# An order planner for TensorE's matmuls, the PSUM banks of the first pass's experts, and the durations the planner assumes

## The chip, the cores and the metric

The kernel runs on one core of a Trainium2 chip. The metric is the time of one execution in microseconds (us) on the device. One execution was also taken with the hardware profiler, and all rows come from that one.

## The reference

Four sequences of 576 tokens with 8 heads of 64 go through retention, a softmax-gated layer with layer norm, and four experts whose outputs are summed with given weights. In short:

```python
scores = (q @ k.T) / sqrt(64)
x = (scores * decay_mask) @ v                    # 2304 tokens x 512
h = x @ w_in                                     # 512 -> 1024
solu = h * softmax(h)
ln = (solu - mean(solu)) / sqrt(var(solu) + 1e-6) * g_ln
x = ln @ w_out                                   # 1024 -> 512
for e in range(4):
    out += p[:, e:e + 1] * (relu(x @ w1[e]) @ w2[e])
```

All is float32. The kernel writes every large matmul as three, on the high and low parts of both operands (`mm3`, line 360).

## The kernel before

The 2304 tokens are 18 groups of 128, in three passes of six groups. A pass has four parts: attention and the first matmul `h_mm` of each group, with its softmax and norm chain on VectorE, ScalarE and GpSimd (`chain1` to `chain3b`) and transposes (`tr`); the second matmul `x2_mm`, whose results are split into sums and differences (`x2_new`); and the four experts. An expert has a first layer `l1` of four steps, each of seven products (a block scheme with seven in place of eight block products), and a second layer `l2_mm` or, in the later passes, two more such steps. Attention for the first eleven groups belongs to pass 0; the other seven groups (11 to 17, the list `OWN`) go beside the last expert's output tiles of pass 0 and beside the first matmuls of pass 1. The code counts passes from 0; the change's title says "pass one" for pass 0.

PSUM has eight banks of 512 f32 columns. In the kernel before, `bt` (b0, b1, b2) and `sbank` hold one each for the whole kernel, and the last four are a pool that is opened again and again: two double tiles `psA0` for pass 0, four single tiles `psX1`, `psX2` for the experts of the later passes (lines 1066 to 1075 and 1249), two double tiles `psA1` between them. `next_a` and `next_b` give these tiles in turn. In pass 0's experts a step takes x from `next_a` and y and z from `next_b` (line 909); products 1, 6, 4 and 7 go to x, 5 and 3 to y, and 2 to z. ScalarE and VectorE read them out: a copy or an add, then a ReLU on ScalarE (`relu_hi`), then its low part on VectorE (`relu_lo`). The second layer's output tiles take `next_b`, and VectorE adds them to `acc` (`l2_out`).

The first part of pass 0, up to about 98 us, is issued in the order of the string `ORDER`, written by hand. From `second(0)` on, instructions are recorded by `Recorder` and emitted at each `flush()`: a region is what lies between two flushes, and all of a region's instructions are emitted before those of the next. `flush` plans a region as a list schedule. Each operation has a cost from `FIXED` and `RATE`, a result reaches another engine after `LATENCY`, DMAs go one after the other at 300 GB/s with 2 us on top, and a PSUM bank takes one engine at a time. An operation's due time is the earlier of two: for a matmul its place on TensorE's clock in recorded order, and for any operation the due times of those that need it, less its cost. An engine takes the ready operation that is due first. TensorE alone may only take the next matmul in recorded order. All these instructions are issued from `op.call()`, so their line in the profile is 144, that of the recorded call; they are told apart by the names of their tiles. In the profile the tiles of `psA0` and `psA1` are psA and those of `psX1` and `psX2` are psX; h is the activation, wA and wC hold weights, wB the second matmul's or an expert's second weights, xa and xb the experts' inputs, tmp and dec attention data or scratch, acc the sums.

Of the kernel before, what the change touches and what calls it, by code (L numbers as in the profile page):

```python
# [59 lines left out]
l4 t5 r3 l5 s1 s3  # L60
"""

LATENCY = 0.12
ISSUE = 0.06
FIXED = {"PE": 0.0135, "ACT": 0.13, "DVE": 0.16, "POOL": 0.36, "SP": 2.0}
RATE = {"PE": 1 / 2400, "ACT": 0.93e-3, "DVE": 1.03e-3, "POOL": 1.82e-3, "SP": 4 * P / 300e3}
# [26 lines left out]
class Recorder:  # L93
# [32 lines left out]
    def record(self, name, engine, kind, args, kw):  # L126
        aps = dict(kw)
        aps.update(zip(("out", "in0", "in1") if kind == "matmul" else ("out", "in_"), args))
        outs = [aps[k] for k in ("out", "accum_out") if isinstance(aps.get(k), bass.AP)]
        keys = ("in_", "in0", "in1", "scalar", "scalar1", "scalar2", "bias", "scale")  # L130
        ins = [aps[k] for k in keys if isinstance(aps.get(k), bass.AP)]
        size = lambda ap: int(np.prod([d[1] for d in tuple(ap.ap)[1:]]))
        n = size(aps["out"])
        if engine == "SP" and aps["out"].space == bass.MemoryType.DRAM:
            n = size(aps["in_"])
        elif kind == "tensor_reduce":
            n = size(aps["in_"])
        rate = RATE[engine]
        if engine == "PE" and aps["in0"].dtype == F32:
            rate *= 2 if kw.get("is_transpose") else 4  # L140
        call = getattr(getattr(self.nc, name), kind)
        wide = [a for a in ins if a.space != bass.MemoryType.PSUM and size(a) > 1]
        port = engine == "POOL" or (engine == "DVE" and len(wide) > 1)
        op = Op(engine, lambda: call(*args, **kw), FIXED[engine] + rate * n, port)  # L144
        op.banks = {a.name for a in ins + outs if a.space == bass.MemoryType.PSUM}
        for a in ins:
            self.note(op, a, False)
        for a in outs:
            self.note(op, a, True)
        op.before.discard(op)  # L150
        op.index = self.count
        self.count += 1
        self.ops.append(op)

    def flush(self, done=True):
        ops, self.ops = self.ops, None if done else []
        clock = max(self.now, self.free["PE"])
        begin = clock
        inside = set(ops)
        for op in ops:  # L160
            op.after, op.due, op.at = [], None, clock
            if op.engine == "PE":
                op.due = clock
                clock += op.cost
        left, ready_at = {}, {}
        for op in ops:
            left[op], ready_at[op] = 0, 0.0
            for b in op.before:
                if b in inside:
                    b.after.append(op)  # L170
                    left[op] += 1
                else:
                    ready_at[op] = max(ready_at[op], b.end + (0 if b.engine == op.engine != "SP" else LATENCY))
        for op in reversed(ops):
            due = min((s.due for s in op.after), default=None)
            if due is None and op.engine != "PE":
                due = op.at + SLACK
            if due is not None:
                due -= op.cost + LATENCY
                op.due = due if op.due is None else min(op.due, due)  # L180
        free, busy = self.free, self.busy
        queue = {e: [] for e in FIXED}
        waiting, order = [], []
        pe = [op for op in ops if op.engine == "PE"]
        at, idle, now = 0, 0.0, self.now
        for op in ops:
            if not left[op]:
                heapq.heappush(waiting, (ready_at[op], op.index, op))
        while len(order) < len(ops):
            late = now + 1e-9  # L190
            while waiting and waiting[0][0] <= late:
                op = heapq.heappop(waiting)[2]
                queue[op.engine].append((op.due, op.index, op))
            moved = False
            for e in FIXED:
                if free[e] > late or not queue[e] or (e == "SP" and self.dma > late + DEPTH):
                    continue
                can = [r for r in queue[e] if not (r[2].port and self.port > late)]
                can = [r for r in can if all(busy.get(b, 0) <= late for b in r[2].banks)]
                if e == "PE":  # L200
                    can = [r for r in can if r[2] is pe[at]]
                if not can:
                    continue
                best = min(can)
                queue[e].remove(best)
                op = best[2]
                moved = True
                if e == "PE":
                    at += 1
                    idle += now - max(free[e], begin)  # L210
                if e == "SP":
                    free[e] = now + ISSUE
                    self.dma = max(self.dma, now) + op.cost - FIXED[e]
                    op.end = self.dma + FIXED[e]
                else:
                    op.end = free[e] = now + op.cost
                if op.port:
                    self.port = op.end
                for b in op.banks:
                    busy[b] = op.end if e == "PE" else op.end + LATENCY  # L220
                op.start = now
                order.append(op)
                for s in op.after:
                    left[s] -= 1
                    ready_at[s] = max(ready_at[s], op.end + (0 if s.engine == e != "SP" else LATENCY))
                    if not left[s]:
                        heapq.heappush(waiting, (ready_at[s], s.index, s))
            if not moved:
                times = [*free.values(), self.port, self.dma - DEPTH, *busy.values(), *(w[0] for w in waiting[:1])]
                now = min(t for t in times if t > late)  # L230
        self.now = min(free.values())
        if TRACE:
            print("scheduled %d from %.1f to %.1f (PE free %.1f) PE idle %.1f" % (len(ops), begin, self.now, free["PE"], idle))
            TRACE.append([(op.start, op.cost, op.engine, op.index, op.due) for op in order])
        for op in order:
            op.call()
# [11 lines left out]

SLACK = 12.0
DEPTH = 2.0  # L250
TRACE = []


@with_exitstack
def retention_solu_moe(
# [32 lines left out]

    bt = [psB.tile([P, 512], F32, tag=f"b{i}", name=f"b{i}") for i in range(3)]
    sbank = psB.tile([P, 512], F32, tag="s", name="sbank")  # L290
    turn = [0]
    open_pool("psA0", 2)

    def next_a():
# [3 lines left out]
    def next_b():  # L298
        turn[0] += 1
        return bt[turn[0] % 3]  # L300

    def quad(t):
        return t.rearrange("p (n t) -> p n t", n=4)
# [601 lines left out]
    def l1(s, i):  # L905

        m = s % NM
        if i == 1:
            x = next_a()[:, 0:BLK]
            y, z = (next_b()[:, 0:BLK] for _ in range(2))  # L910
            steps[s] = (x, y, z)
        x, y, z = steps[s]
        if i == 1:
            prod(s, 1, x)
            copy(t1r, x)
            if m > 0:
                relu_hi(1, m + 3, c22)
                relu_lo(1, m + 3, c22)
        elif i == 5:
            prod(s, 5, y)  # L920
            copy(t5r, y)
        elif i == 2:
            prod(s, 2, z)
            add(z, z, t1r)
        elif i == 6:
            prod(s, 6, x, True)
            copy(t2r, x)
            relu_hi(0, m, z)
            relu_lo(0, m, z)
        elif i == 3:  # L930
            prod(s, 3, y, True)
            add(y, y, t2r)
        elif i == 7:
            prod(s, 7, x, True)
            add(c22, x, t5r)
            relu_hi(1, m, y)
            relu_lo(1, m, y)
            if m == NM - 1:
                relu_hi(1, m + 4, c22)
                relu_lo(1, m + 4, c22)  # L940
        elif i == 4:
            prod(s, 4, x, True)
            relu_hi(0, m + 4, x)
            relu_lo(0, m + 4, x)
            steps.pop(s)
# [23 lines left out]
    def experts(p):  # L969
        for e in range(E):  # L970
# [9 lines left out]
                        l1(s - 1, 4)  # L980
                        w1_next(s + 2)
            last = s0 + NM - 1
            first = next_b()
            l2_mm(first, 1, 0, FORDER[:2], True, False)
            l1(last, 4)
            w1_next(last + 3)
# [10 lines left out]
            for b in (1, 0):  # L997
                for t in range(TB):
# [1 line left out]
                        ps, first = first, None  # L1000
                        l2_mm(ps, b, t, FORDER[2:], False, True)
                    else:
                        ps = next_b()
                        l2_mm(ps, b, t, FORDER, True, True)
                    l2_out(p, e, b * TB + t, ps)
                    if e + 1 == E:
# [59 lines left out]
    def experts_s(p):  # L1066
# [179 lines left out]
                        x_load(p + 1, g)  # L1246
        nc.flush()
        if p + 1 < NPASS:
            open_pool(f"psA{p}", 2)
            nc.start()  # L1250

    OWN = list(range(EARLY, NG))
# [32 lines left out]
    def second(p, g0):  # L1285

        if p == 0:
            raw = tmp[:, 2048:3072]
            w1_load(0)
            w1_load(1, raw)  # L1290
            xb_region()
            nc.start()
            w1_ops(0)
            w1_ops(1, raw)
# [20 lines left out]
    with tc.manual_schedule():  # L1315
# [43 lines left out]
            atoms[atom[0]](int(atom[1:]))  # L1359
        second(0, None)  # L1360
        experts(0)
        for p in range(1, NPASS):
            g0 = p * GP
            own = p == 1
# [119 lines left out]
```

## Time and profile before

| | us |
|---|---|
| median of 3 runs (1037.69 to 1041.31) | 1039.89 |
| profiled execution | 1042.08 |
| its span, first to last instruction | 1040.3 |
| TensorE busy | 1008.3 |
| VectorE busy | 617.3 |
| ScalarE busy | 526.9 |
| GpSimd busy | 445.6 |
| HBM traffic | 169.00 MB read, 62.95 MB written |

PE is TensorE's matmul, PEld its weight load (it overlaps matmuls), DVE is VectorE, ACT is ScalarE, POOL is GpSimd and SP is SyncE, which issues all DMAs. A row of a timeline has start, length, engine, source line, operation, out<-in, shapes and count, and in brackets the idle time before it and what ended it. Matmuls overlap each other in the rows, since each is shown with its whole latency: matmuls begin faster than one row's mean length suggests.

### The profile page before, as it was taken

The numbers are of one execution on the slowest core, as the hardware profiler recorded it, in microseconds if no ns is written. First come the engines' busy times: TensorE is split into PE (matmuls) and PEld (weight loads), VectorE is DVE, ScalarE is ACT, GpSimd is POOL, SyncE is SP. The second block draws the span as 40 slices with busy tenths as digits, with TensorE's granted clock in tenths as the row PEclk, the third lists the DMA queues.
The fourth block names the chain that finished last, engine by engine and source line by source line (L and its number), as shares of the span: only waits on it lengthen the run. The fifth ranks groups of instructions, "written<-read, shape, count | busy, mean of one in ns | idle before, by whom it ended". The sixth has DMA issues, their size and how long they took to land.

```text
span 1040.3 us, 17080 instructions
## 1 busy us (share of the span) xinstructions
PE 1008.3 (97%) x6188; PEld 947.0 (91%) x6188; DVE 617.3 (59%) x1038; ACT 526.9 (51%) x1032; POOL 445.6 (43%) x433
## 2 busy tenths in 40 slices
PE   4899999999999999999999999999999999999998
PEld 3788998898988987889999999999899999999998
DVE  6999686585774513643735656475444636556564
ACT  4568664262533402563745556473573746555462
POOL 2333354333635011321465655654230465655553
PEclk9999999999999999999999999999999999999999
DMA  9857689999785858551757666577640847566524
GB/s 343 343 186 257 216 293 313 309 292 336 227 270 185 280 226 304 203 200 59 232 152 226 184 195 211 157 270 248 243 152 18 250 134 244 163 216 193 184 72 134
DMA packets 122788, 226.79 MB, mean 218 GB/s; under 512 B 9936, under 2 KB 57040, under 8 KB 116560
## 3 DMA queue, kind: packets, MB, share of 16 engines
q1 hardware_dynamic: 122704, 225.70, 65.2%
q8 instruction: 49, 0.80, 0.3%
q14 instruction: 35, 0.29, 0.1%
HBM read 169.00 MB, written 62.95 MB: 223 GB/s over the span
## 4 chain that ended last, share of the span: by engine, by line
PE 51%; issue 1%; DVE 0%; ACT 0%; POOL 0%; POOLq 0%; ACTq 0%
PE psX L144 26%; PE b L144 16%; PE sbank L144 6%; PE psA L144 3%; DVE acc L144 0%; POOL acc L144 0%; DVE stats L144 0%; ACT psA L144 0%; ACT acc L144 0%; DVE tmp L144 0%; ACT xb L144 0%; ACT xa L144 0%; ACT tmp L144 0%; POOLq L144 0%; ACTq L144 0%
## 5 line engine op out<-in xcount | busy, mean ns | idle before, releaser
L144 POOL TENSOR_TENSOR h<-tmp,h 128x384 fp32r<-128x384 f32 x128 | 128.7, 1015 | 95.9 <-ACT h L144 82.1
L144 PE MATMUL b<-xa,wA 128*128 128x384 f32 x672 | 132.8, 335 | 2.3 <-DVE h L144 1.2
L144 PE MATMUL b<-wB,h 128*128 128x512 f32 x576 | 133.0, 390 | 1.3 <-POOL wB L144 1.3
L144 PEld LDWEIGHTS b<-wB,h 128*128 128x128 f32 x576 | 107.8, 188 | 24.2 <-POOL wB L144 2.2
L144 POOL TENSOR_TENSOR wA<-wA 128x512 fp32r<-128x512 f32 x74 | 97.2, 1321 | 68.0 <-ACT wA L144 65.0
L144 PEld LDWEIGHTS b<-xa,wA 128*128 128x128 f32 x672 | 117.7, 188 | 3.5 <-DVE h L144 2.1
L144 PE MATMUL psX<-xb,wA 128*128 128x384 f32 x576 | 112.6, 336 | 0.1
L144 PEld LDWEIGHTS psX<-xb,wA 128*128 128x128 f32 x576 | 100.4, 188 | 2.7 <-DVE b L144 2.3
L144 POOL TENSOR_TENSOR tmp<-tmp 128x256 f32<-128x256 f32 (+1 forms) x68 | 61.9, 925 | 72.0 <-DMA tmp<-in_w 50.0
L144 ACT ACTIVATE h<-tmp 128x384 fp32r<-128x384 f32 x144 | 72.9, 521 | 33.7 <-DVE tmp L144 33.7
L144 PE MATMUL b<-h,wB 128*128 128x384 f32 x480 | 85.1, 336 | 0.0
L144 PEld LDWEIGHTS b<-h,wB 128*128 128x128 f32 x480 | 83.0, 188 | 0.1
L144 PE MATMUL psX<-h,wA 128*128 128x384 f32 x408 | 74.9, 334 | 0.0
L144 DVE TENSOR_TENSOR sbank<-sbank,tmp 128x384 f32<-128x384 f32 x48 | 27.2, 566 | 77.4 <-PE sbank L144 54.3
L144 ACT ACTIVATE wA<-wA 128x512 fp32r<-128x512 f32 x74 | 46.3, 632 | 51.5 <-DMA wA<-sw 41.7
L144 ACT ACTIVATE tmp<-b 128x384 f32<-128x384 f32 x104 | 51.1, 491 | 41.8 <-DVE b L144 17.1
L144 PEld LDWEIGHTS psX<-h,wA 128*128 128x128 f32 x408 | 71.1, 188 | 0.0
L144 PE MATMUL psA<-wA,xa 128*128 128x512 f32 x288 | 70.2, 399 | 0.8 <-DVE tmp L144 0.7
L144 DVE TENSOR_TENSOR b<-b,tmp 128x384 f32<-128x384 f32 x80 | 45.0, 563 | 41.1 <-PE b L144 38.0
L144 PEld LDWEIGHTS psA<-wA,xa 128*128 128x128 f32 x288 | 53.6, 190 | 13.3 <-DVE tmp L144 1.0
L144 POOL TENSOR_TENSOR wC<-wC 128x512 fp32r<-128x512 f32 x38 | 50.6, 1337 | 31.8 <-ACT wC L144 31.8
L144 DVE SCALAR_TENSOR_TENSOR tmp<-b,tmp 128x384 f32<-128x384 f32 x96 | 51.2, 554 | 16.9 <-ACT tmp L144 8.5
(239 smaller groups left out, 1984.4 us busy)
## 6 DMA issues: line engine op xcount, KB each, us to landing
wA<-sw SPq DMA_DIRECT2D x298, 256.0 KB, 3.0
sw<-wA SPq DMA_DIRECT2D x32, 896.0 KB, 7.7
tmp<-in_w SPq DMA_DIRECT2D x24, 512.0 KB, 5.7
grps<-in_qkv SPq DMA_DIRECT2D x10, 1024.0 KB, 6.5
wC<-sw SPq DMA_DIRECT2D x38, 256.0 KB, 2.8
sw<-wCf SPq DMA_DIRECT2D x32, 256.0 KB, 3.3
wA<-sin SPq DMA_DIRECT2D x8, 1024.0 KB, 6.7
wB<-sout SPq DMA_DIRECT2D x8, 1024.0 KB, 8.0
```

The costliest lines, as they stand in the source:

```text
L144: op = Op(engine, lambda: call(*args, **kw), FIXED[engine] + rate * n, port)
```

## The change

The planner lets TensorE take, among the ready matmuls, the one that is due first, as long as it was recorded at most `AHEAD` = 150 operations (of any engine) behind the first matmul not yet issued. The assumed durations change: `LATENCY` from 0.12 to 0.15 us, f32 matmuls that are not transposes from four to two times a column's cost, and VectorE operations with two wide operands in SBUF to 1.2 times theirs. In pass 0's experts the two double tiles are given back before the region of `second(0)`, four single tiles `psX0` are opened, and x, y, z and the output tiles take all seven banks (three b, four psX0) in turn with `next_x`. Behind pass 0's experts there is a new flush, after which two double tiles `psA1` are opened for pass 1; those of pass 2 are now named `psA2`.

```diff
--- before.py
+++ after.py
@@ -60,7 +60,7 @@
 l4 t5 r3 l5 s1 s3
 """
 
-LATENCY = 0.12
+LATENCY = 0.15
 ISSUE = 0.06
 FIXED = {"PE": 0.0135, "ACT": 0.13, "DVE": 0.16, "POOL": 0.36, "SP": 2.0}
 RATE = {"PE": 1 / 2400, "ACT": 0.93e-3, "DVE": 1.03e-3, "POOL": 1.82e-3, "SP": 4 * P / 300e3}
@@ -137,10 +137,11 @@
             n = size(aps["in_"])
         rate = RATE[engine]
         if engine == "PE" and aps["in0"].dtype == F32:
-            rate *= 2 if kw.get("is_transpose") else 4
+            rate *= 2
         call = getattr(getattr(self.nc, name), kind)
         wide = [a for a in ins if a.space != bass.MemoryType.PSUM and size(a) > 1]
         port = engine == "POOL" or (engine == "DVE" and len(wide) > 1)
+        rate *= 1.2 if engine == "DVE" and port else 1.0
         op = Op(engine, lambda: call(*args, **kw), FIXED[engine] + rate * n, port)
         op.banks = {a.name for a in ins + outs if a.space == bass.MemoryType.PSUM}
         for a in ins:
@@ -158,7 +159,7 @@
         begin = clock
         inside = set(ops)
         for op in ops:
-            op.after, op.due, op.at = [], None, clock
+            op.after, op.due, op.at, op.start = [], None, clock, None
             if op.engine == "PE":
                 op.due = clock
                 clock += op.cost
@@ -198,7 +199,9 @@
                 can = [r for r in queue[e] if not (r[2].port and self.port > late)]
                 can = [r for r in can if all(busy.get(b, 0) <= late for b in r[2].banks)]
                 if e == "PE":
-                    can = [r for r in can if r[2] is pe[at]]
+                    while at < len(pe) and pe[at].start is not None:
+                        at += 1
+                    can = [r for r in can if r[2].index <= pe[at].index + AHEAD]
                 if not can:
                     continue
                 best = min(can)
@@ -206,7 +209,6 @@
                 op = best[2]
                 moved = True
                 if e == "PE":
-                    at += 1
                     idle += now - max(free[e], begin)
                 if e == "SP":
                     free[e] = now + ISSUE
@@ -248,6 +250,7 @@
 
 SLACK = 12.0
 DEPTH = 2.0
+AHEAD = 150
 TRACE = []
 
 
@@ -288,7 +291,7 @@
 
     bt = [psB.tile([P, 512], F32, tag=f"b{i}", name=f"b{i}") for i in range(3)]
     sbank = psB.tile([P, 512], F32, tag="s", name="sbank")
-    turn = [0]
+    turn = [0, 0]
     open_pool("psA0", 2)
 
     def next_a():
@@ -298,6 +301,10 @@
     def next_b():
         turn[0] += 1
         return bt[turn[0] % 3]
+
+    def next_x():
+        turn[1] += 1
+        return (bt + pool["a"])[turn[1] % 7]
 
     def quad(t):
         return t.rearrange("p (n t) -> p n t", n=4)
@@ -906,8 +913,7 @@
 
         m = s % NM
         if i == 1:
-            x = next_a()[:, 0:BLK]
-            y, z = (next_b()[:, 0:BLK] for _ in range(2))
+            x, y, z = (next_x()[:, 0:BLK] for _ in range(3))
             steps[s] = (x, y, z)
         x, y, z = steps[s]
         if i == 1:
@@ -980,7 +986,7 @@
                         l1(s - 1, 4)
                         w1_next(s + 2)
             last = s0 + NM - 1
-            first = next_b()
+            first = next_x()
             l2_mm(first, 1, 0, FORDER[:2], True, False)
             l1(last, 4)
             w1_next(last + 3)
@@ -1000,7 +1006,7 @@
                         ps, first = first, None
                         l2_mm(ps, b, t, FORDER[2:], False, True)
                     else:
-                        ps = next_b()
+                        ps = next_x()
                         l2_mm(ps, b, t, FORDER, True, True)
                     l2_out(p, e, b * TB + t, ps)
                     if e + 1 == E:
@@ -1246,7 +1252,7 @@
                         x_load(p + 1, g)
         nc.flush()
         if p + 1 < NPASS:
-            open_pool(f"psA{p}", 2)
+            open_pool("psA2", 2)
             nc.start()
 
     OWN = list(range(EARLY, NG))
@@ -1289,6 +1295,7 @@
             w1_load(0)
             w1_load(1, raw)
             xb_region()
+            open_pool("psX0", 4)
             nc.start()
             w1_ops(0)
             w1_ops(1, raw)
@@ -1359,6 +1366,9 @@
             atoms[atom[0]](int(atom[1:]))
         second(0, None)
         experts(0)
+        nc.flush()
+        open_pool("psA1", 2)
+        nc.start()
         for p in range(1, NPASS):
             g0 = p * GP
             own = p == 1
```

## Rows read from the trace of the kernel before

**Rows 1.** The page, part 1: busy time and share of each engine.

```profile
PE 1008.3 (97%) x6188; PEld 947.0 (91%) x6188; DVE 617.3 (59%) x1038; ACT 526.9 (51%) x1032; POOL 445.6 (43%) x433
```

**Rows 2.** Table by stretches: length, busy time (count) by engine, clock, DMA.

```profile
0.00:98.00 98.00, 79.59 (x790) 66.26 (x791) 84.73 (x111) 59.33 (x109) 35.70 (x39) 0.98 0.79 294
98.00:385.00 287.00, 282.84 (x1486) 257.03 (x1485) 182.21 (x300) 123.16 (x238) 107.85 (x105) 1.00 0.81 268
385.00:460.00 75.00, 71.67 (x646) 59.87 (x646) 34.26 (x57) 29.25 (x52) 15.48 (x24) 0.98 0.57 209
...
500.00:727.00 227.00, 227.00 (x1306) 225.84 (x1305) 129.33 (x235) 125.94 (x261) 130.52 (x114) 1.00 0.66 210
727.00:804.00 77.00, 75.07 (x401) 67.90 (x401) 36.65 (x66) 40.28 (x69) 15.65 (x26) 1.00 0.37 137
```

**Rows 3.** Chain that ended last, 750 to 805 us: start, length, what.

```profile
753.07 5.47 PE psA L144 x24
...
780.04 20.82 PE b L144 x120
```

**Rows 4.** Waits of TensorE: us in total, times, longest.

```profile
PE sbank L144 <- POOL tmp L144: 2.4, 1, 2.4
...
PE b L144 <- POOL wB L144: 1.3, 2, 0.7
PE b L144 <- DVE h L144: 1.2, 2, 0.7
...
PE psA L144 <- DVE h L144: 1.1, 1, 1.1
PE b L144 <- ACT xb L144: 1.1, 1, 1.1
PE b L144 <- DVE tmp L144: 0.9, 2, 0.7
PE psA L144 <- DVE tmp L144: 0.7, 1, 0.7
PE psA L144 <- ACT tmp L144: 0.5, 1, 0.5
```

**Rows 5.** Timeline, 284 to 289 us: start, length, instructions, idle before.

```profile
285.68 1.21 PE L144 MATMUL b<-xa,wA 128*128 128x384 f32 x6
...
287.55 1.31 PE L144 MATMUL b<-xa,wA 128*128 128x384 f32 x6 [0.66 <-DVE h L144]
```

**Rows 6.** Timeline, 355 to 412 us.

```profile
389.69 1.01 SPq L144 DMA_DIRECT2D wB<-sout  x2
...
394.32 0.37 SPq L144 DMA_DIRECT2D tmp<-in_qkv  x1
...
395.36 1.16 PE L144 MATMUL b<-dec 64*128 64x128 f32 x16
...
402.70 1.04 POOL L144 TENSOR_TENSOR tmp<-tmp,tabs 128x512 f32<-128x512 f32 x1 [23.83 <-DMA tmp<-in_qkv]
...
403.80 0.68 PE L144 MATMUL sbank<-tmp 128*64 128x64 f32 x16 [2.42 <-POOL tmp L144]
...
404.41 1.96 PE L144 MATMUL b<-tmp 64*128 64x128 f32 x16
```

**Rows 7.** Table by stretches, 400 to 420 us.

```profile
400.00:420.00 20.00, 17.58 (x164) 14.74 (x161) 8.33 (x13) 6.17 (x11) 6.57 (x9) 0.91 0.79 305
```

**Rows 8.** DMA issues: KB each, median us from issue to landing.

```profile
tmp<-in_w SPq DMA_DIRECT2D x24, 512.0 KB, 5.7
...
tmp<-in_qkv SPq DMA_DIRECT2D x4, 1024.0 KB, 6.6
```

**Rows 9.** Timeline, 722 to 732 us.

```profile
725.61 2.25 PE L144 MATMUL psX<-h,wC 128*128 128x384 f32 x12
...
727.89 0.56 DVE L144 TENSOR_TENSOR tmp<-psX,pb 128x384 f32<-128x384 f32 x1 [0.26 <-PE psX L144]
...
728.50 3.68 PE L144 MATMUL psA<-wA,xa 128*128 128x512 f32 x15 [0.65 <-DVE tmp L144]
```

## The prediction

> **What bounds the kernel now.** I read the page's busy shares first: TensorE is busy for 97% of the span, VectorE, the next, for 59% [rows 1]. So only two things can move the time: the work of TensorE, which the change leaves alone, and the moments in which TensorE does not issue. The table by stretches places them [rows 2]. Up to 98 us TensorE is idle for 18.4 us, but that stretch is issued in an order written by hand, which the change does not touch. From 98 to 385 us (the end of the second matmul of pass zero and its experts; "pass one" in the change's title) 4.2 us are idle, from 385 to 460 us 3.3 us, from 727 to 804 us 1.9 us. In the experts of the later passes, 500 to 727 us for instance, it is busy for all of 227.00 us.
>
> Busy is not yet peak, so I read the issue rate: 120 matmuls of 384 columns in 20.82 us, 24 of 512 columns in 5.47 us, so 173.5 and 228 ns each [rows 3]. The planner assumes 0.0135 us and one column per cycle of 2.4 GHz: 173.5 and 226.8 ns. Where it does not wait, TensorE runs at the planner's own price, and nothing is to be had there. What is to be had are the waits themselves.
>
> **The sum of the stalls.** The list of waits has 12 of TensorE behind 98 us; eight of its rows stand in [rows 4] and add to 9.2 us (the ninth, of 0.2 us, is an evicted psA). The view counts idle time from the modelled end of a matmul and is short by the overlap: six matmuls that begin at 285.68 need 6 x 173.5 ns = 1.04 us, the next could begin at 286.72 and begins at 287.55, 0.83 us later, where the row says 0.66 [rows 5]. I add 0.17 us to each of the 12: 9.4 + 2.0 = 11.4 us. One stall costs more: after TensorE stood for 2.42 us at 401 us [rows 6], the granted clock over 400 to 420 us is 0.91 of 2.4 GHz, so some 3.6 us lay at 1.2 GHz, and the same 16 matmuls took 1.96 us where they take 1.16 us at full clock [rows 6, 7]. I put that at 1.3 us, an estimate between the 0.8 us of those matmuls and half of 3.6 us. All stalls behind 98 us: 12.7 us, or 1.2% of the span. That is the most that the change can give back.
>
> **The change part by part.**
> *Seven banks.* In pass zero's experts a step holds three banks: x from two double tiles in turn, y and z from b0 to b2. A step's z lies where the step before had its y. [Rows 5] show the price: product 2 of a step waits for VectorE's second half of the ReLU of the step before, on the same bank. With seven in turn two successive steps share none. This takes the waits b <- DVE h (2) and psA <- DVE h (1) of [rows 4]: 1.2 + 1.1 + 3 x 0.17 = 2.8 us. Who is next late there? The following matmul's operands are in SBUF since long and its bank is free; I see nothing behind it.
> *Look-ahead.* The planner may now give TensorE any ready matmul up to 150 recorded operations behind the first one not yet issued, by due time. It can fill the waits that come from a chain of evictions: psA <- ACT tmp, b <- DVE tmp (2), b <- ACT xb: 0.5 + 0.9 + 1.1 + 4 x 0.17 = 3.2 us. There is work to fill them with: at the last of these product 2 reads another operand and is ready. I take all 3.2 us. The two waits b <- POOL wB (1.3 + 0.34 = 1.6 us) hang on a weight load; the plan can only dodge what it foresees, and it prices a 512 KB load at 2.0 + 1.75 = 3.75 us, where the median is 5.7 us [rows 8]. Half: 0.8 us. The waits psA <- DVE tmp and psA <- ACT psA (0.7 + 0.2 + 0.34 = 1.2 us) stay: the first is that of a region's first matmul for a bank just given back, the second has little ready work beside it.
> *The extra flush behind pass zero's experts, and the pool opened there.* The operations of the experts' last six output tiles are now all emitted before those of pass 1. This moves DMAs: in the kernel before, two loads of wB for pass 1 (1 MB each) were issued at 389.69, ahead of the load of tmp at 394.32 for attention group 13; it landed 8.3 us later, GpSimd's multiply followed at 402.70, and TensorE waited for that until 403.80 [rows 6]. Now the flush puts the tmp load ahead of all four wB loads on SP's queue. At its median of 6.6 us [rows 8] it is there 1.7 us earlier, and h_mm(6, 1), 12 x 0.228 = 2.7 us, may go ahead of the wait. wB is first read after the six tiles' h, far behind. The stall and its clock stretch are worth 2.4 + 0.17 + 1.3 = 3.9 us; I take 3.0. The new pool itself: at 728.50 such a hand-over cost 0.65 + 0.17 = 0.8 us [rows 9]; here the experts ask for 4 x 18 = 72 banks in turn, so the last three output tiles lie in b0 to b2, and psX0's banks have been free for 3 x 24 x 0.228 = 16 us. I cost it at nothing, at most 0.8 us. Without that cover h_mm(6, 0) would wait for the last eviction. Opening psX0 before the first step lies behind four second matmuls of 24 x 0.1735 = 4.2 us each: nothing either.
> *Durations.* LATENCY goes from 0.12 to 0.15 us, f32 matmuls from four to two cycles per column, VectorE with two SBUF operands to 1.2 times the rate. 16 score matmuls are now planned at 1.92 us, before at 3.6 us, and take 1.16 us [rows 6]: nearer. No instruction gets faster by it.
> *What it may cost.* TensorE's order is still fixed once planned. A matmul that the plan puts right at a hand-over loses what the plan is short of. From the last of 12 matmuls (725.61 + 11 x 0.1735 = 727.52, planned end 727.69) to VectorE at 727.89 there are 0.20 us, the plan says 0.15; from VectorE's end at 728.45 to TensorE at 728.50 there are 0.05, the plan says 0.15 [rows 9]. So an edge costs from -0.10 to +0.05 us. The trace of before does not show how many edges there will be; with one at each of 64 expert steps (16 in pass zero, 48 later) the price is -6 to +3 us; a gain is out where TensorE has no idle time, so 0 to 3 us, and since edges on loads are dearer I take the upper end, 3 us. Behind a TensorE that waits stand all later matmuls, and the evictions that free weight slots for SP's loads.
> Sum: 2.8 + 3.2 + 0.8 + 3.0 - 3.0 = 6.8 us less. The profiled execution took 1042.08 us, 1.8 us more than its span and 2.2 us above the median of the runs, 1039.89. So 1035.3 us for an execution like it, and 1033.1 us for the median: I forecast 1033.
>
> One rule speaks against seven banks. In this trace idle moments of TensorE up to 1.1 us behind 98 us [rows 4] left the granted clock at 1.00 over 98 to 385 us and 727 to 804 us [rows 2]; only the one of 2.42 us was followed by half clock. The Trainium skill, "TensorE: Matmul & The Clock Gate", section "A second HAM failure mode: psum-queue depth-cycling", tells of a kernel that cycled through PSUM banks, idled briefly between groups of matmuls, and saw its clock fall again and again. The trace here does not agree as far as it goes.
>
> **The rivals.**
> *All is filled.* The plan's durations fit the rows to some per cent, so every stall but the 1.2 us could go without new ones: 12.7 - 1.2 = 11.5 us, 1028. Against it: two stalls hang on loads.
> *Nearly nothing moves.* If the plan does not see the stalls (it would have to, to fill them), only the banks' 2.8 us remain, less some edges: 1037 to 1040, say 1038. For it: the largest stall comes from a load priced too low. Against it: the bank waits go by construction.
> *Slower: matmuls planned onto loads that come late.* TensorE takes matmuls earlier, nearer to their loads; a 512 KB weight load comes 2.0 us later than planned [rows 8]. There are 32 such loads in pass zero. Each matmul group set on that edge stops TensorE for up to 2.0 us; from 5 edges on the gain of 9.8 us is eaten, at 8 the time is 1039.9 - 9.8 + 16 = 1046. Against it: in the kernel before only two waits are on weights, and a later matmul has a later due time.
> *The clock.* If short idles at seven banks' hand-overs brought half clock, each would cost about 1.3 us as at 404 us; ten of them on top of the banks' gain give 1040 - 2.8 + 13 = 1050. That is the page's rule as a mechanism here.
>
> **How the numbers follow.** Forecast (1031 to 1036.8, at 1033): 0.43. All filled (1027 to 1031): 0.18. Nearly nothing (1036.8 to 1042): 0.26. Late loads (1043 to 1048): 0.10. Clock: 0.03. A measurement of this kernel can tell 0.3%, 3.1 us, from no change: faster is below 1036.8, slower above 1043.0. So faster 0.61, same 0.26, slower 0.13. The range of 8 in 10 leaves out the last two cases and the far end of the second: 1028 to 1042.
>
> **What would show it.** In the profile after, the waits of TensorE for DVE h in pass zero should be gone (banks), those for ACT xb and DVE tmp too (look-ahead); the tmp load should precede the wB loads, and the granted clock around 400 us should be 1.00. TensorE's idle time behind 98 us should fall from 9.4 us to 4 or 5. The stretch up to 98 us should last as before. I am wrong if new waits of TensorE appear in the experts of the later passes, where there was none, or waits for POOL wB or a DMA in pass zero grow.

## The result, and the profile after

The changed kernel takes 1046.21 us (median of 6 runs, 1045.74 to 1048.49), the kernel before, measured beside it, 1040.6 us: a ratio of 1.0058, with a 95% interval from 1.0039 to 1.0077. It is slower by some 6 us, where 7 us less were forecast. The profiled execution took 1046.01 us and spans 1044.2.

Most of TensorE's waits are gone, as predicted. These are the waits that its list has behind 98 us in the changed kernel, but for one of 0.2 us (us in total, times, longest); [rows 4] had 9.2 us there, these add to 2.8:

```profile
PE psA L145 <- DVE tmp L145: 1.2, 1, 1.2
PE psX L145 <- DVE tmp L145: 0.9, 1, 0.9
...
PE psX L145 <- ACT tmp L145: 0.5, 2, 0.3
...
PE sbank L145 <- POOL wC L145: 0.2, 1, 0.2
```

But TensorE is busy for longer with the same 6188 matmuls, 1020.6 us against 1008.3 [rows 1]. The page's first part, after:

```profile
PE 1020.6 (98%) x6188; PEld 951.5 (91%) x6188; DVE 617.4 (59%) x1038; ACT 526.4 (50%) x1032; POOL 443.4 (42%) x433
```

To place it I cut both traces where the same work begins: at the first `x2_mm` of pass 0, the first `h_mm` of pass 1, and so on, by the start of the first matmul of each (the last row ends at the start of its last matmul). Lengths in us (e1 and e7 are experiments told below):

| stretch | before | after | e1 | e7 |
|---|---|---|---|---|
| first x2_mm of pass 0 to h_mm of pass 1 | 298.8 | 295.7 | 292.5 | 292.5 |
| h_mm to x2_mm of pass 1 | 61.6 | 69.1 | 60.7 | 58.8 |
| x2_mm of pass 1 to its experts | 35.3 | 36.2 | 35.3 | 35.3 |
| experts of pass 1 | 235.2 | 236.2 | 233.8 | 233.8 |
| h_mm and x2_mm of pass 2 | 72.2 | 72.5 | 72.2 | 72.2 |
| experts of pass 2 | 235.2 | 233.5 | 232.8 | 232.8 |

Pass 0 gives 3.1 us and the last experts 1.7. One stretch takes 7.5 us: that in which pass 1's first matmuls run beside attention. Here is the table by stretches for just that stretch (length, then busy time and count of PE, PEld, DVE, ACT, POOL, the granted clock, DMA share, GB/s), first of the kernel before:

```profile
396.45:458.01 61.56, 58.23 (x514) 48.45 (x513) 30.06 (x51) 25.94 (x44) 15.48 (x24) 0.97 0.56 208
```

and after the change:

```profile
391.72:460.83 69.11, 69.11 (x506) 50.63 (x505) 31.43 (x51) 27.34 (x46) 15.54 (x24) 1.00 0.55 209
```

There is no idle moment left, no half clock, eight matmuls fewer fall into it, and TensorE is busy for 10.9 us longer. VectorE and ScalarE are busy for 1.4 us longer at most. (The eight matmuls are transposes; they fall into the next stretch.) The timeline of TensorE there shows why (start, length, operation, out<-in, shapes, count):

```profile
396.58 0.50 PE L145 MATMUL psA<-wA,xa 128*128 128x512 f32 x1
397.01 0.43 PE L145 MATMUL b<-dec,st 128*64 128x128 f32 x2
397.37 0.51 PE L145 MATMUL psA<-wA,xa 128*128 128x512 f32 x1
397.81 0.48 PE L145 MATMUL b<-tmp 64*128 64x128 f32 x2
398.22 0.50 PE L145 MATMUL psA<-wA,xa 128*128 128x512 f32 x1
398.65 0.71 PE L145 MATMUL b<-tmp 64*128 64x128 f32 x6
399.29 0.51 PE L145 MATMUL psA<-wA,xa 128*128 128x512 f32 x1
399.73 0.73 PE L145 MATMUL sbank<-tmp 128*64 128x64 f32 x16
```

Each line is a change between attention's small matmuls (which use 64 rows or 64 columns of the array) and `h_mm`'s of 512 columns. From one start to the next a single 512-column matmul takes 0.43 us (398.22 to 398.65, 397.37 to 397.81 0.44), where it takes 0.228 in a run [rows 3]; two score matmuls take 0.41 us (397.81 to 398.22), where 16 in a run take 1.09 us to the start of the next matmul, so two 0.14. In the kernel before, the same work stood in whole runs:

```profile
414.69 1.16 PE L144 MATMUL b<-dec 64*128 64x128 f32 x16
415.78 5.76 PE L144 MATMUL psA<-wA,xa 128*128 128x512 f32 x24
421.47 1.09 PE L144 MATMUL b<-dec 128*64 128x128 f32 x16
422.39 1.04 PE L144 MATMUL b<-dec,st 128*64 128x128 f32 x16
```

I counted the places where a matmul of 384 or 512 columns is followed by one of fewer ("entries" below): 9 in this stretch before, 44 after; behind 98 us 22 and 83. Of the 35 more in the stretch, 8 lead into transposes, for which e6 below finds no price, and 27 into attention's matmuls (6 before, 33 after). 10.9 us over these 27 are 0.40 us each.

The planner does this by itself, without any wait: two lists of ready matmuls whose due times overlap (`h_mm`'s go up by 0.227 us from one to the next) are merged by due time, one by one. To the planner a matmul costs the same wherever it stands.

Two steps of the prediction can be seen here too. SP issues the load of tmp ahead of those of wB (timeline of SP, after):

```profile
390.52 0.34 SPq L145 DMA_DIRECT2D tmp<-in_qkv  x1
391.18 0.73 SPq L145 DMA_DIRECT2D tmp<-in_qdec  x1
391.95 0.43 SPq L145 DMA_DIRECT2D wB<-sout  x1
```

and GpSimd can begin 5.0 us after the issue, where it was 8.4 [rows 6]:

```profile
395.56 1.04 POOL L145 TENSOR_TENSOR tmp<-tmp,tabs 128x512 f32<-128x512 f32 x1 [19.17 <-DMA tmp<-in_qkv]
```

### The profile page after: what moved, and what is told of

The parts are those of the page before. It is cut to its first block, busy times and chain, and to the rows that moved or that the text cites. A ratio compares the mean times of both kernels' runs of the same rounds, so it can differ in the third digit from the quotient of the medians.

```text
span 1044.2 us, 17088 instructions
## 1 busy us (share of the span) xinstructions
PE 1020.6 (98%) x6188; PEld 951.5 (91%) x6188; DVE 617.4 (59%) x1038; ACT 526.4 (50%) x1032; POOL 443.4 (42%) x433
## 4 chain that ended last, share of the span: by engine, by line
PE 90%; DVE 4%; DMA 3%; ACT 1%; issue 1%; SPq 0%; POOL 0%; ACTq 0%; DVEq 0%; POOLq 0%
PE psX L145 37%; PE b L145 35%; PE psA L145 7%; PE sbank L145 7%; DMA dec<-in_w_in 1%; DMA wC<-sw 1%; DMA sx<-wA 1%; PE b L370 1%; PE psA L370 1%; PE psA L371 1%; PE b L372 1%; PE b L371 1%; PE psA L372 1%; PE b L595 0%; PE b L589 0%
## 5 line engine op out<-in xcount | busy, mean ns | idle before, releaser
L145 PE MATMUL psX<-xb,wA 128*128 128x384 f32 x720 | 198.4, 335 | 1.2 <-DVE tmp L145 0.9
L145 PE MATMUL b<-xa,wA 128*128 128x384 f32 x552 | 161.3, 334 | 0.0
L145 PEld LDWEIGHTS psX<-xb,wA 128*128 128x128 f32 x720 | 131.3, 188 | 2.9 <-DVE tmp L145 1.4
L145 PE MATMUL psX<-xa,wA 128*128 128x384 f32 x408 | 112.0, 335 | 0.0
L145 PE MATMUL psX<-h,wA 128*128 128x384 f32 x408 | 104.3, 335 | 0.3 <-ACT tmp L145 0.3
L145 ACT ACTIVATE tmp<-psX 128x384 f32<-128x384 f32 x121 | 59.0, 488 | 71.6 <-PE psX L145 70.4
L145 PE MATMUL psX<-wB,h 128*128 128x512 f32 x312 | 82.2, 390 | 0.0
L145 PEld LDWEIGHTS psX<-xa,wA 128*128 128x128 f32 x408 | 74.5, 188 | 0.3
L145 PE MATMUL b<-wB,h 128*128 128x512 f32 x264 | 70.4, 391 | 0.0
L145 PEld LDWEIGHTS psX<-wB,h 128*128 128x128 f32 x312 | 58.5, 188 | 11.6
```

## The experiments

Theory I: mixing the two kinds costs TensorE time, and that is the loss. Theory II: the loss comes with the new region border and pool, or with other orders of the other engines. The ratio of each run is to the kernel before, measured beside it, with its 95% interval.

**e1: recorded order first.** TensorE looks ahead only when the next matmul in recorded order is not ready.

```diff
                     can = [r for r in can if r[2].index <= pe[at].index + AHEAD]
+                    can = [r for r in can if r[2] is pe[at]] or can
```

> The changed kernel, but TensorE takes the next matmul in recorded order whenever that one is ready, and looks ahead only when it is not. Theory I (mixing costs: the planner merges the 128-column attention matmuls of pass 1 with the 512-column ones of h_mm by due time, and each change between the two kinds costs TensorE about 0.2 us on top of the matmul): the stretch from the first h_mm of pass 1 to the first x2_mm of pass 1, 61.6 us before and 69.1 after the change, falls to 57 to 60 us, and the time is 1029 to 1035 us. Theory II (the new region border and the pool opened there cost the time, or other orders of VectorE and SP): the stretch stays at 67 us or more and the time at 1044 to 1047 us.

1030.57 us, ratio 0.9921 (0.9905 to 0.9938). The stretch is 60.7 us, with 18 entries; border, pool, banks and durations are all still there. The time is theory I's; the stretch is 0.7 us above its 57 to 60 us, with no idle moment and nine more entries than before, all into attention's matmuls.

```profile
391.31:451.98 60.67, 60.67 (x515) 48.06 (x513) 31.14 (x52) 26.93 (x46) 15.54 (x24) 1.00 0.65 236
```

**e2: whole groups.** Choice by due time as in the change, but TensorE stays with a run once begun.

```diff
+        run, last = 0, None
+        for a, b in zip([None] + pe, pe):
+            if a is None or a.kind != b.kind or b.index != a.index + 1 or (b.kind == "r" and a.banks != b.banks):
+                run += 1
+            b.run = run
...
+                    can = [r for r in can if r[2].run == last] or can
```

> The changed kernel, with choice by due time and look-ahead of 150 as it is, but TensorE stays with the group of matmuls it has begun (one run of attention matmuls or transposes, or one PSUM tile's products) as long as its next matmul is ready. Theory I (mixing costs): entries into small matmuls fall from 83 behind 98 us to about 25, the stretch from h_mm to x2_mm in pass 1 is 57 to 60 us, and the time 1029 to 1035 us. Theory II (border and pool): 1044 to 1047 us. If reordering of whole groups is itself harmful, the stretch is short but later stretches stay longer than before, 1037 to 1042 us.

1033.98 us, ratio 0.9944 (0.9928 to 0.996); 22 entries behind 98 us, 11 in the stretch, which is 59.3 us. The reordering itself does little harm; against e1 its profiled execution has new waits for evictions by ScalarE and VectorE, 1.4 us for ACT h and 1.9 for DVE h, about the difference of the two medians.

**e3: banks and border only.** The kernel before with the seven banks, the flush and the pool, TensorE in recorded order, old durations.

```diff
-            x = next_a()[:, 0:BLK]
-            y, z = (next_b()[:, 0:BLK] for _ in range(2))
+            x, y, z = (next_x()[:, 0:BLK] for _ in range(3))
...
+        nc.flush()
+        open_pool("psA1", 2)
+        nc.start()
```

> The kernel before with the seven banks, the extra flush and the pool opened there, but TensorE in recorded order and the old durations. Theory I: the waits for DVE h in pass 0 are gone, 2.8 us, and the wait for the tmp load at 401 us is shorter, up to 3.9 us: 1034 to 1038 us, and the stretch from h_mm to x2_mm in pass 1 is 57 to 62 us. Theory II: that stretch is 66 us or more and the time 1043 us or more.

1040.07 us, ratio 1.0001 (0.9991 to 1.0012): nothing either way, so theory I's 1034 to 1038 us were not reached. The stretch is 58.8 us, so theory II's border and pool are not the loss. The waits b <- DVE h are gone (2.3 us with that of psA), but the list of waits has new ones of pass 0 in their place, for DVE xa, DVE acc and (0.4 us) DVE h; the rest of these rows stood in [rows 4] too:

```profile
PE psX L144 <- POOL wB L144: 1.5, 2, 0.8
...
PE b L144 <- ACT xb L144: 1.1, 1, 1.1
PE b L144 <- DVE xa L144: 1.1, 1, 1.1
PE b L144 <- DVE tmp L144: 0.9, 2, 0.8
PE b L144 <- DVE acc L144: 0.8, 1, 0.8
```

**e4: look-ahead only**, by due time, on the kernel before.

```diff
-                    can = [r for r in can if r[2] is pe[at]]
+                    while at < len(pe) and pe[at].start is not None:
+                        at += 1
+                    can = [r for r in can if r[2].index <= pe[at].index + AHEAD]
```

> The kernel before with the look-ahead of 150 alone: old banks, no extra flush, old durations. Theory I: small matmuls are mixed with 512-column ones in pass 1, entries into small matmuls behind 98 us rise from 22 to 60 or more, the stretch from h_mm to x2_mm in pass 1 is 65 us or more, the time 1040 to 1050 us. Theory II: without border and pool the look-ahead only fills waits: 1031 to 1036 us.

1048.71 us, ratio 1.0082 (1.0067 to 1.0097); 78 entries behind 98 us, 40 in the stretch, which is 68.2 us and all busy. The look-ahead by due time alone makes the whole loss.

```profile
394.18:462.40 68.22, 68.22 (x515) 51.08 (x515) 30.86 (x51) 26.25 (x45) 15.52 (x24) 1.00 0.50 186
```

**e5: mixing put into e1.** Score matmuls and `h_mm(g, 1)` recorded in turn for five groups.

```diff
-                    att_first(OWN[i + 2])
-                h_mm(g, 1)
+                    att_st(OWN[i + 2])
+                    mixed(lambda: att_qk(OWN[i + 2]), lambda: h_mm(g, 1), 2)
+                    att_ret(OWN[i + 2])
+                    att_state(OWN[i + 2])
```

> The kernel of e1 (recorded order first), but for five attention groups of pass 1 the 16 score matmuls (64 rows) and the 12 matmuls of 512 columns of h_mm(g, 1) are recorded in turn, two and one: seven more entries into small matmuls for each group, 35 in all, nothing else. Theory I (mixing costs): in the changed kernel a pair of score matmuls and one of 512 columns took 0.84 us where they take 0.36 us unmixed, so 35 x 0.48 = 17 us more than e1 at most, and 10 us if the cost is the mean of that kernel: the stretch from h_mm to x2_mm in pass 1 rises from 60.7 to between 70 and 78 us, the time from 1030.6 to 1040 to 1048 us. If the mixing was only a companion of some other loss: 1030 to 1032 us.

1035.69 us, ratio 0.9958 (0.9941 to 0.9974), 5.1 us over e1, below what was expected. The dose was smaller than meant: a recorded f32 matmul is issued as two, so the 16 score matmuls of a group are 8 recorded ones and 15 more entries were put in, not 35; and the look-ahead took other ready matmuls, so that 5 were left (23 in the stretch, e1 18). The stretch is 63.5 us, 2.9 more than e1's, 0.6 of it a wait for a DMA; the rest of the 5.1 us does not lie there. Of the profiled execution's part 1.6 us lie in pass 0 (294.1 us against 292.5), where TensorE's order is the same as in e1: a wait of 1.3 us for DVE h, ahead of the mixing. With the same order there e6 and e10 have it too (1.0 us), e1 and e7 have not: scatter from execution to execution. In the stretch TensorE is busy for 62.92 us against e1's 60.67, 0.45 us for each of the 5 entries.

**e6: transposes mixed.** As e5, but with the f32 transposes of pass 2, which use the whole array.

```diff
-                h_mm(g, 1)
+                if i > 1 and not own:
+                    mixed(lambda: t_mm(g - 2), lambda: h_mm(g, 1), 1)
```

> The kernel of e1, but for four groups of pass 2 the eight f32 transposes (128 rows and 128 columns of the array) and the 12 matmuls of 512 columns of h_mm(g, 1) are recorded in turn, one and one: 28 more entries into small matmuls. Theory Ia (what costs is the change between matmuls on the whole array and matmuls on half of its rows or columns): in the changed kernel transposes and 512-column matmuls in turn took no longer than one after the other, so the time stays at 1030 to 1033 us. Theory Ib (what costs is the change of type between f32 and fp32r, or any change of shape): 28 x 0.35 = 10 us more, 1038 to 1042 us, and the stretch from h_mm to x2_mm in pass 2 rises from 37.0 to about 47 us.

1033.05 us, ratio 0.9937 (0.9913 to 0.9961), 2.5 us over e1, with an interval that overlaps e1's. 53 entries behind 98 us, 22 more than in e1, and the stretch from h_mm to the experts of pass 2 is 72.7 us against 72.2. TensorE's timeline:

```profile
734.55 0.27 PE L145 MATMUL b<-tabs,acc 128*128 128x128 f32 x1
734.58 0.48 PE L145 MATMUL psA<-wA,xa 128*128 128x512 f32 x1
734.89 0.27 PE L145 MATMUL b<-tabs,acc 128*128 128x128 f32 x1
734.92 0.48 PE L145 MATMUL psA<-wA,xa 128*128 128x512 f32 x1
```

A transpose and a 512-column matmul together take 0.34 us from start to start (734.55 to 734.89), and 0.228 plus the 0.109 us that a transpose takes in a run make the same. Changes between matmuls that both use the whole array cost nothing here.

**e7: same kind.** e1, but what is taken out of order is of the kind of the matmul before (attention or not), if such a one is ready.

```diff
-                    can = [r for r in can if r[2] is pe[at]] or can
+                    same = [r for r in can if r[2].small == small]
+                    can = [r for r in can if r[2] is pe[at]] or same or can
```

> The kernel of e1, but a matmul taken out of order is of the same kind as the one before (attention or not) where such a one is ready. e1 has 31 entries into small matmuls behind 98 us, the kernel before 22; nine entries less at 0.3 us would be 2.7 us: 1028 to 1030 us. If the entries that e1 still has fill real waits, nothing is won: 1030 to 1032 us.

1029.12 us, ratio 0.9894 (0.9874 to 0.9913): the fastest of all, faster than both kernels, though its interval meets e1's. 25 entries behind 98 us; the stretch is 58.8 us against 60.7 in e1. There, in the profiled execution, TensorE waits again, 1.28 us for the tmp load, and the stretch is still 1.9 us shorter than the one that e1 filled:

```profile
394.45 1.16 PE L145 MATMUL b<-tmp 64*128 64x128 f32 x16 [1.28 <-DMA tmp<-in_qkv]
395.54 0.51 PE L145 MATMUL psA<-wA,xa 128*128 128x512 f32 x1
```

**e8: the kernel before with e1's look-ahead alone**, old banks, no border, old durations (the lines of e4 and of e1).

> The kernel before with the look-ahead alone, and that only when the next matmul in recorded order is not ready: old banks, no extra flush, old durations. If the look-ahead is what gives the gain of e1, it fills the bank waits too: 1031 to 1034 us. If the banks and the border carry half of it: 1034 to 1037 us.

1032.9 us, ratio 0.9932 (0.9912 to 0.9952): the look-ahead alone gives most of e1's gain. Not all waits are filled: its list still has 1.5 us for POOL tmp and 1.2 for DVE h.

**e9: mixing put into the kernel before**, strictly in recorded order (the edit of e5).

> The kernel before, strictly in recorded order, but for five attention groups of pass 1 the 16 score matmuls and the 12 matmuls of h_mm(g, 1) are recorded in turn, two and one: 35 more entries into small matmuls, and no look-ahead that could undo them (in e5 only five remained). Theory I: in the changed kernel a single 512-column matmul among attention matmuls took 403 ns, 176 more than in a run, and two score matmuls between such ones 389 ns, some 260 more: 35 x 0.44 = 15 us, so the stretch from h_mm to x2_mm in pass 1 rises from 61.6 to 73 to 78 us and the time to 1051 to 1056 us. If e1's gain over the changed kernel came from anything else than mixing: 1038 to 1043 us.

1045.09 us, ratio 1.0048 (1.003 to 1.0066). The expectation rested on the same wrong count of 35; there are 24 entries in the stretch, 15 more than before. At the 0.44 us expected for each, 15 would be 6.6 us; the time rose by 5.0. The timeline of one group:

```profile
401.26 0.49 PE L144 MATMUL b<-tmp 64*128 64x128 f32 x4
401.68 0.50 PE L144 MATMUL psA<-wA,xa 128*128 128x512 f32 x1
402.11 0.49 PE L144 MATMUL b<-tmp 64*128 64x128 f32 x4
...
403.82 0.49 PE L144 MATMUL b<-tmp 64*128 64x128 f32 x4
404.24 5.05 PE L144 MATMUL psA<-wA,xa 128*128 128x512 f32 x21
```

16 score and three 512-column matmuls take 2.98 us (401.26 to 404.24); unmixed they would take 1.09 + 3 x 0.228 = 1.77. That is 0.40 us for each of the three entries, in recorded order and with no look-ahead. In the profiled execution the stretch grew by only 1.9 us, since two waits of the kernel before became shorter on the way and no half clock fell into it (the granted clock is 1.00 there).

**e10: ordinary f32 matmuls on the whole array.** e6 with pass 2's transposes done as matmuls with the identity.

```diff
-                nc.tensor.matmul(tps[g][u][:, f], src, ident, start=f == 0, stop=f == 3, is_transpose=True)
+                nc.tensor.matmul(tps[g][u][:, f], src, ident, start=f == 0, stop=f == 3, skip_group_check=True)
```

> The kernel of e6, but the transposes of pass 2 are done as ordinary f32 matmuls with the identity (128 rows, 128 columns, the whole array), four groups mixed one to one with the 512-column matmuls of h_mm and two groups of eight unmixed. Theory Ia (half of the array): mixed, such a matmul and a 512-column one together take their unmixed times, within 0.05 us. Theory Ib (ordinary f32 against fp32r): together they take 0.2 to 0.45 us more than unmixed, as attention matmuls do.

Its time (1039.91 us, one execution) is not the point, since these matmuls are slower than transposes; the rows are. Mixed, then unmixed:

```profile
737.16 0.38 PE L145 MATMUL b<-tabs,acc 128*128 128x128 f32 x2
737.30 0.48 PE L145 MATMUL psA<-wA,xa 128*128 128x512 f32 x1
737.61 0.38 PE L145 MATMUL b<-tabs,acc 128*128 128x128 f32 x2
...
753.37 1.83 PE L145 MATMUL b<-tabs,acc 128*128 128x128 f32 x14
754.95 0.48 PE L145 MATMUL psA<-wA,xa 128*128 128x512 f32 x1
```

Two instructions (one recorded matmul) and one of 512 columns take 0.45 us mixed (737.16 to 737.61); unmixed, 1.58 / 7 = 0.226 and 0.228 add to 0.45. So f32 beside fp32r (the type that the kernel gives its wide matmuls) costs nothing on the whole array. What attention's matmuls have besides is that they use 64 rows or 64 columns; that this is the cause is what is left, not what a run changed by itself.

The weight loads say more of where the time goes. First from the changed kernel, beside the timeline above, then from e10:

```profile
397.80 0.29 PEld L145 LDWEIGHTS b<-tmp 64*128 64x128 f32 x2 [0.25 <-issue]
398.22 0.19 PEld L145 LDWEIGHTS psA<-wA,xa 128*128 128x128 f32 x1
...
737.38 0.42 PEld L145 LDWEIGHTS b<-tabs,acc 128*128 128x128 f32 x2
```

In e10 the load for the pair that starts at 737.61 begins 0.23 us ahead, beside the wide matmul that started at 737.30. In the changed kernel both loads begin with their own matmuls (397.81, 398.22), so nothing of them lies beside the matmul before. In its trace all 78 changes behind 98 us between attention's matmuls and the others are so, to 0.003 us. Matmuls that run side by side would not explain the price alone: on the whole array two f32 instructions take 0.226 us in a run, and the pair between two changes takes 0.41.

**e11: runs of attention matmuls kept whole**, all other choices as in the change.

```diff
+            if a is None or not (a.small and b.small) or b.index != a.index + 1:
+                run += 1
...
+                    can = [r for r in can if r[2].run == last] or can
```

> The changed kernel with choice by due time and look-ahead, but TensorE stays with a run of attention matmuls as long as its next one is ready; transposes and products are mixed as in the changed kernel. If mixing of attention matmuls alone is the loss: the stretch from h_mm to x2_mm in pass 1 falls from 69.1 to 58 to 61 us and the time to 1032 to 1036 us. If mixing of the other kinds costs too: 1037 to 1041 us.

1035.97 us, ratio 0.997 (0.9955 to 0.9985), 10.2 us under the changed kernel. The stretch is 58.4 us. With transposes and products still mixed 62 entries are left behind 98 us, 26 of them in the stretch (14 into attention's matmuls), and the stretch is shorter than e1's. The 5 us to e1 do not lie there: in the profiled executions the experts of pass 1 take 236.4 us against 233.8 and pass 0 294.1 against 292.5, and choice by due time keeps two waits for DVE tmp that the changed kernel has (0.9 and 1.2 us). The rest is not placed.

**e12: durations only**, on the kernel before.

```diff
-LATENCY = 0.12
+LATENCY = 0.15
...
-            rate *= 2 if kw.get("is_transpose") else 4
+            rate *= 2
...
+        rate *= 1.2 if engine == "DVE" and port else 1.0
```

> The kernel before with the new assumed durations alone. In recorded order TensorE can only lose or win waits by them: 1037 to 1042 us, no difference that can be told. If the durations by themselves spoil the order of VectorE and SP: 1043 us or more.

1037.51 us, ratio 0.9973 (0.9958 to 0.9989): a small gain where none was expected to be told. The wait for the tmp load is 1.7 us in place of 2.4, and the granted clock in the stretch is 1.00 (0.97 before):

```profile
393.24:451.15 57.91, 56.21 (x514) 46.94 (x513) 30.43 (x51) 25.90 (x44) 15.50 (x24) 1.00 0.60 217
```

**The price over all runs.** TensorE's busy time in the stretch, all at a granted clock of 1.00, beside the entries into attention's matmuls there:

| run | e12 | e8 | e3 | e7 | e2 | e11 | e1, e6 | e5 | e9 | e4 | after |
|---|---|---|---|---|---|---|---|---|---|---|---|
| entries | 6 | 6 | 6 | 9 | 9 | 14 | 15 | 20 | 21 | 31 | 33 |
| busy, us | 56.2 | 56.9 | 57.1 | 57.5 | 58.9 | 58.4 | 60.7 | 62.9 | 62.1 | 68.2 | 69.1 |

Against the mean of the first three, 56.7 us, the last five columns (e1 to after) give 0.36 to 0.46 us for each entry added. For e7, e2 and e11 the scatter among the first three, 0.9 us, is too large to read a price from. (In the changed kernel and e11 eight transposes, some 0.9 us, fall outside the stretch.)

## Why the prediction was wrong

*The step that failed* is the first sentence of the bound: "the work of TensorE, which the change leaves alone". The number of matmuls stayed, their time did not. The part on what the change may cost looked for new waits at hand-overs, priced them at 0 to 3 us, and had no term for the order itself; by 27 entries at 0.40 us it was 10.9 us, and 12.4 against the 56.7 us that the same stretch is busy at full clock. The sum stood at 9.8 us of gain less 3, and the waits that it counted did go; the 10.9 us ate all of it. The rows could have warned: the 16 score matmuls in [rows 6] take 1.16 us as a run, 0.07 each, where a transpose of 128 columns on the whole array takes 0.109: so matmuls on part of the array follow another price than the planner's, and what a wide matmul between them does was worth a question. And I treated look-ahead as something that acts only on a wait, though the code takes the earliest due time always; e1 against the changed kernel, 1030.57 against 1046.21 us, is that one line.

*The stalls* were counted about right: 9.4 us of waits behind 98 us fell to 3.0, further than the 4 or 5 I named, the granted clock of the stretch is 1.00, and the tmp load goes ahead of wB with 5.0 us in place of 8.4. So look-ahead, flush and clock were right as mechanisms. For the flush I took 3.0 us; e3's profiled stretch is 2.8 us shorter. The half clock I put at 1.3 us; it cost about 1.5 (58.23 us busy against 56.7). But I took it off the median, and it does not seem to fall into every execution: of the 29 of the kernel before that were measured beside e12, ten have a mean granted clock of 0.996 or less and a median of 1041.8 us, the other 19 one of 1038.6. One sign that I had named against me did come, and is small: three new waits in the experts of the later passes, 0.8 us in all. The look-ahead term was too small: e8 gives 6.6 to 7 us without banks or border. Some of that lies where I said nothing is to be had: the experts of passes 1 and 2 are 1.4 and 2.4 us shorter in e1 (of the 2.4 us 1.3 are the wait for ACT xb that I had counted). The view of waits leaves out gaps under 0.15 us. In the kernel before a wait of that kind stands in each expert of pass 1, as between the seventh of these matmuls, which would end its turn at 522.11 + 7 x 0.1735 = 523.32, and the next one at 523.46:

```profile
522.11 1.38 PE L144 MATMUL psX<-wB,wA 128*128 128x384 f32 x7
523.46 1.32 PE L144 MATMUL psX<-xb,wA 128*128 128x384 f32 x6
```

*The banks' term* of 2.8 us was wrong by itself: I saw "nothing behind" the waits for DVE h, and e3 shows new waits for VectorE in their place (1.1 + 0.8 + 0.4 us) and no gain. With the look-ahead, banks, border and durations together make the 2.3 us between e8 and e1, which their intervals do not tell apart.

*The durations* I costed at nothing; alone they gave 2.5 us in e12 (1.1 to 4.4 by its interval). My arithmetic on them was off too: 16 score matmuls are 8 recorded ones, planned at 0.96 us after and 1.81 before, against 1.16 us.

*The rivals*: neither late loads nor the clock made the kernel slower. No wait for a weight load longer than 0.2 us is left behind 98 us, and the clock did not fall there. The slower rivals had the right sign and the wrong place; the one that came true was not among them, and that the late loads were priced at 1046 us is chance. The page of the Trainium skill that I weighed, "TensorE: Matmul & The Clock Gate", section "A second HAM failure mode: psum-queue depth-cycling", tells of a fall of the clock that no run here shows for the banks: with seven in turn, and waits up to 1.2 us, the granted clock is 1.00 from 98 to 1039 us.

What stays open is why the weight load does not go ahead at these changes; no run took that apart. Whether the 64 are rows or columns makes no difference that the changed kernel's rows show: a wide matmul takes 0.43 us between two of 64 rows (14 places) and between two of 64 columns (9 places).

## What to carry to other kernels

A scheduler that may reorder matmuls needs a price for the change between matmuls on part of the array and on the whole of it, or it will merge two streams one by one: let it keep to the recorded order and look ahead only on a wait, and then prefer the kind that is running. When an engine is the bound, ask not only what it waits for but whether the same instructions in another order take the same time. A short wait can be cheaper than the work that fills it (e7).

## What the runs showed of the hardware

A 512-column matmul on the whole array between matmuls on 64 rows or 64 columns took 0.43 us where it takes 0.228 in a run, and a pair of those on 64 rows 0.41 us where it takes 0.14 (after). Over whole stretches a change there and back cost 0.36 to 0.46 us (e1, e4, e5, e9, after). At these changes the weight load began with its own matmul; between matmuls on the whole array it began while the one before ran (after, e10). Between a 512-column matmul and f32 matmuls or transposes on the whole array, the change cost nothing that the rows show (0.34 and 0.45 us, mixed as unmixed; e6, e10). An f32 matmul of 128 columns that is no transpose is issued as two instructions and takes 0.226 us on the whole array, a transpose 0.109.
